# PE in program order while attention runs beside the first expert layer, and ELU's parts marked urgent there

## Chip, core and metric

The kernel runs on one core of one Trainium2 chip. Its engines are PE (TensorE, the matmuls, with PEld for the loads of the stationary operand), DVE (VectorE), ACT (ScalarE), POOL (GpSimd) and SP (SyncE, which here only issues DMAs). The metric is device time in microseconds of one execution, lower is better.

## What is computed

Three stages follow each other. The first is a linear attention with decay over two batches of 8 heads, 768 positions and head size 64, written for blocks of 64:

```python
for b in range(nb):
    qb, kb, vb = (q[:, :, sl], k[:, :, sl], v[:, :, sl])
    intra = np.einsum('bhic,bhjc->bhij', qb, kb) * Dmask[None]
    intra = np.einsum('bhij,bhjd->bhid', intra, vb)
    inter = np.einsum('bhid,bhde->bhie', qb * lam_pow[None], kv_state)
    out[:, :, sl] = intra + inter
    kv_state = lam_block * kv_state + np.einsum('bhsd,bhse->bhde', kb_dec, vb)
```

Its output, reshaped to 1536 tokens of 512, goes through two dense layers of inner size 2048, the first with ELU and the second with softplus:

```python
h = x @ w_in;  g = np.where(h > 0.0, h, np.exp(np.minimum(h, 0.0)) - 1.0);  x = g @ w_out
h = x @ w_in2; g = np.maximum(h, 0.0) + np.log1p(np.exp(-np.abs(h)));      x = g @ w_out2
```

## The kernel before

Attention works on 12 chunks g of 128 positions (all 8 heads; chunks 0 to 5 are the first batch), and has three kinds of matmul groups on PE, eight or sixteen small matmuls each, that use the 128 x 128 array in three different forms. `s(g)`, line 228, multiplies k with q (64 rows by 128 columns of the array); `t(g)`, line 272, makes the state from k and v (128 rows by 64 columns); `x(g)`, lines 245 and 250, makes the output, first from the state (64 by 64), then from the scores (128 by 64). DVE masks the scores (line 231), adds the state (278), and splits the output into a high and a low part together with ACT (xh on ACT, line 260; xl on DVE, line 261). POOL scales q in place after s(g) (203), ACT scales k and v's partner k for the state (209, head by head).

A dense layer goes over 3 tiles of 512 tokens and 16 pieces of the inner size, 48 steps n. `m1(n)`, lines 343 to 345, is 12 matmuls of 512 columns that need the split token tile and weight chunk n's high and low part; ELU follows (`pointwise1` on ACT, `pointwise2` on DVE line 378, ACT line 383 and POOL line 384); `m2(n)`, line 408, is 12 more matmuls, issued two steps later. These use the whole array. Steps 0 to 3 work on token tile 0 (chunks 0 to 3), steps 4 to 7 on tile 1 (chunks 4 to 7) with the same weight chunks 0 to 3.

A weight chunk arrives as float64 words and is converted by two operations on ACT and six on DVE (lines 98 to 120; the last is line 120, which writes the low part). Eight chunks are converted while attention runs; weight chunks 4 to 7 are used only later. In the traces' names wh_215 belongs to chunk 0, wh_271 to 1, wh_343 to 2, wh_413 to 3, and wl_482 to 4.

A scheduler orders the instructions of an engine, except inside `manual_schedule`, where the engines that are named keep the order in which the code is written. The first part (setup, 13 attention slots, then steps 0 to 7) keeps only SP in the order of the code; from step 8 on PE, ACT, POOL and SP keep it. `high_priority(k)` makes the scheduler prefer what stands under it. A step's code is: a slot t, m1(n), its ELU, a slot s, m2(n-2), a slot x. SP's queue is in the order of the code in both kernels: the load of weight chunk k+2 waits until line 120 of chunk k has run, and the loads of later q, k and v stand behind it.

Of the kernel before, what the change touches and what calls it, by code (L numbers as in the profile page):

```python
# [1 line left out]

# [1 line left out]

# [32 lines left out]
def body(ctx, tc, lamc, ident, attqk, attkv, w1, w2, out):  # L37
# [41 lines left out]
    def w_ops(count, start):  # L79

        while count:
            if not flight:
                if not start or wnext[1] == len(wqueue):
                    return
                flight.append(split_w(wqueue[wnext[1]]))
                wnext[1] += 1
            if next(flight[0], True):
                flight.pop()
            count -= 1
# [44 lines left out]
    def setup():  # L134
        A.preload_act_table_set("natural_log_exp_and_others")
        V.memset(zero, 0.0)

        ps = ps_h.tile([P, TT], F32, tag="h", name="warm")
        for i in range(9):
            T.matmul(ps[:, :P], zero, zero, start=True, stop=True)  # L140
        nc.sync.dma_start(out=lam_t, in_=lamc)
        nc.sync.dma_start(out=id_t, in_=ident)
        att_load(0)
        att_load_kv(0)
        load_w()
        att_load(1)
        att_load_kv(1)
        for g in (2, 3):
            att_load(g)
            att_load_kv(g)  # L150
        load_w()

    def decays():
        for h in range(H):
            V.tensor_tensor_scan(
                out=dmask[:, h % 2, h // 2, :], data0=lam_t[:, h:h + 1].to_broadcast([P, P]), data1=id_t,
                initial=0.0, op0=ALU.mult, op1=ALU.add,
            )
        for e in range(2):
            V.tensor_copy(kdecay[:, e::2], dmask[:, e, :, P - 1])  # L160
        for p in range(NPAIR):
            V.tensor_tensor_scan(
                out=qpow[:, p, :], data0=lam_t[:, H + p:H + p + 1].to_broadcast([P, P]), data1=zero,
                initial=1.0, op0=ALU.mult, op1=ALU.add,
            )
# [39 lines left out]
    def att_prep_k(g):  # L205
        if g < NCHUNK and g % CPB < CPB - 1:
            for h in range(H):
                k = at[g][2][:, D * h:D * h + D]
                A.activation(out=k, in_=k, func=AF.Copy, scale=kdecay[:, h:h + 1])
# [82 lines left out]
    def flush():  # L292
        while deferred:
            deferred.pop(0)()

    def att_slot(ahead=None):

        with tc.high_priority(ahead):
            att_part()
# [32 lines left out]
    def m1(n):  # L332
        u, c = order[n]
        layer, t, begin, _ = units[u]
        fc = layer * NF + c
        if c == begin:
            xcur[u % 2] = (xh[t], xl[t])
        h, l = xcur[u % 2]
        pool, tag = (ps_a, "a") if late and n % 2 else (ps_h, "h")
        ps = pool.tile([P, TT], F32, tag=tag, name="hps")  # L340
        for k in range(KD):
            o = slice(P * k, P * k + P)
            T.matmul(ps, wh[fc, 0][:, o], h[:, k, :], start=(k == 0), stop=False)  # L343
            T.matmul(ps, wh[fc, 0][:, o], l[:, k, :], start=False, stop=False)  # L344
            T.matmul(ps, wl[fc, 0][:, o], h[:, k, :], start=False, stop=(k == KD - 1))  # L345
        return ps


    mid = {}

    def pointwise1(n, ps):
        if units[order[n][0]][0] == 0:
            v = tp.tile([P, TT], F32, tag="v", name="v")
            A.activation(out=v, in_=ps, func=AF.Relu, scale=-1.0)  # L354
            A.activation(out=v, in_=v, func=AF.Exp, scale=-1.0)  # L355
            mid[n] = ps, v, None
        else:

            lp = late["tp"]
            e = lp.tile([P, TT], F32, tag="e", name="e")  # L360
            l = lp.tile([P, TT], F32, tag="l", name="l")
            u = lp.tile([P, TT], F32, tag="u", name="u")
            A.activation(out=e, in_=ps, func=AF.Abs)  # L363
            A.activation(out=e, in_=e, func=AF.Exp, scale=-1.0)
            A.activation(out=u, in_=e, func=AF.Copy, bias=1.0)
            A.activation(out=l, in_=u, func=AF.Ln)  # L366
            mid[n] = ps, l, (u, e)

    def pointwise1b(n):
        if n in mid and mid[n][2]:  # L370
            u, e = mid[n][2]
            V.scalar_tensor_tensor(out=u, in0=u, scalar=-1.0, in1=e, op0=ALU.add, op1=ALU.subtract)  # L372

    def pointwise2(n):
        ps, v, u = mid.pop(n)
        if u is None:

            V.scalar_tensor_tensor(out=v, in0=v, scalar=-1.0, in1=ps, op0=ALU.add, op1=ALU.max)  # L378
        else:
            V.tensor_tensor(out=v, in0=v, in1=u[0], op=ALU.subtract)  # L380
            V.scalar_tensor_tensor(out=v, in0=ps, scalar=0.0, in1=v, op0=ALU.max, op1=ALU.add)
        g = gp.tile([P, 2, TT], F32R, tag="g", name="g")
        A.activation(out=g[:, 0], in_=v, func=AF.Copy)  # L383
        G.tensor_tensor(out=g[:, 1], in0=v, in1=g[:, 0].bitcast(F32), op=ALU.subtract)  # L384
        gt[n] = g

    split = []
    ahead = []

    def split_x():  # L390
        if split:
            t, y, m = split.pop(0)
            A.activation(out=xh[t][:, m, :], in_=y, func=AF.Copy)
            G.tensor_tensor(out=xl[t][:, m, :], in0=y, in1=xh[t][:, m, :].bitcast(F32), op=ALU.subtract)
# [49 lines left out]
    def close_attention():  # L444
        actx.close()
        late["acc"] = ctx.enter_context(tc.tile_pool(name="late", bufs=1, reuse_waits="tile"))
        late["tp"] = ctx.enter_context(tc.tile_pool(name="ltp", bufs=2, reuse_waits="tile"))

    def w_start(n):

        j = n - 13
        return wnext[1] < 8 or j >= 0 and j % 2 == 0 and j % 24 < 16

    def step(n):
        last = len(order) - 1
        pieces = 4 if n < 4 else 2
        att_slot(100)
        if n <= last:
            pointwise1(n, ahead.pop() if ahead else m1(n))
        if n == last - 1:  # L460
            ahead.append(m1(last))
        if n - 1 in mid:
            pointwise2(n - 1)
        if n <= last:
            pointwise1b(n)
        split_x()
        w_ops(pieces, wnext[1] < 8)
        att_slot(100)
        if n >= LAG:
            m2(n - LAG)  # L470
        att_slot(100)
        flush()
        if not slots and not late:
            close_attention()
        w_ops(pieces, w_start(n))

    ET = mybir.EngineType


    with tc.manual_schedule(engines={ET.SP}):  # L480
        setup()
        decays()
        att_prep_k(0)
        while len(slots) > 3 * (NCHUNK - TT // P) - 1:
            if not spare:
                spare.extend([f"y{m}" for m in range(KD)])
            att_slot()
            w_ops(2, True)
        spare.clear()
        for n in range(8):  # L490
            step(n)
    with tc.manual_schedule(engines={ET.PE, ET.Activation, ET.Pool, ET.SP}):
        for n in range(8, len(order) + LAG):
            step(n)
# [47 lines left out]
```

## Time and profile before

| | us |
|---|---|
| median of 3 runs | 636.27 (635.71 to 636.72) |
| the profiled execution, own time | 634.41 |
| its span, first to last instruction | 632.6 |
| PE busy | 610.4 |
| DVE busy | 408.5 |
| ACT busy | 341.1 |
| POOL busy | 173.6 |

The own time is 1.8 us above the span, and 1.9 us below the median of the runs. Busy PE is no measure of PE at its peak: a matmul counts as busy while the engine changes the form of the array or runs at half its clock.

### The profile page before, as it was taken

To read this page: it belongs to the slowest core of one execution; us is meant where nothing else is said; L and a number is where in the kernel's file an instruction comes from. 1 tells how busy PE (TensorE), PEld (TensorE's weight loads), DVE (VectorE), ACT (ScalarE), POOL (GpSimd) and SP (SyncE) were. 2 spreads that over 40 slices of the span, in tenths; PEclk is the share of its full clock that TensorE was granted. 3 is DMA by queue.
4 is the path that set the end of the run, shared out by engine and by line. 5 is a ranking of instruction groups with operands and counts; after the bars stand their busy time and mean duration, and the time that the engine had idled before them with its cause. 6 is when DMAs were issued, how large, how long until landed. Compare 5 with 4: busy or idle time off the path is not lost.

```text
span 632.6 us, 7785 instructions
## 1 busy us (share of the span) xinstructions
PE 610.4 (96%) x3026; PEld 495.7 (78%) x3026; DVE 408.5 (65%) x469; ACT 341.1 (54%) x577; POOL 173.6 (27%) x130
## 2 busy tenths in 40 slices
PE   7979879999999999999999998999999999999997
PEld 6666667788888888888888886888878888888885
DVE  6387992311275867221787899556999996555654
ACT  4435462334356554333556677466787775655553
POOL 1222221212223222224335235322223232222222
PEclk9669966999999999999999999999999999999999
DMA  8505465100013231100113213000231300100101
GB/s 318 218 20 223 192 265 184 51 0 1 0 68 117 84 132 68 66 1 1 67 68 129 75 62 111 23 1 1 71 129 67 132 2 1 67 1 1 67 0 67
DMA packets 10117, 49.86 MB, mean 79 GB/s; under 512 B 1248, under 2 KB 1376, under 8 KB 5984
## 3 DMA queue, kind: packets, MB, share of 16 engines
q1 hardware_dynamic: 10080, 49.36, 21.0%
q8 instruction: 24, 0.39, 0.3%
q14 instruction: 13, 0.11, 0.0%
HBM read 46.21 MB, written 3.15 MB: 78 GB/s over the span
## 4 chain that ended last, share of the span: by engine, by line
PE 82%; issue 6%; DVE 5%; ACT 2%; POOL 2%; DMA 1%; SPq 0%; POOLq 0%; DVEq 0%; ACTq 0%
PE y L408 37%; PE hps L345 13%; PE hps L343 13%; PE hps L344 13%; PE sps L228 3%; PE xps L245 2%; PE xps L250 1%; PE stps L272 1%; POOL g L384 1%; DMA qk<-attqk 1%; DVE t L109 1%; POOL qk L203 1%; DVE wl L120 1%; DVE u L372 1%; DVE raw L99 1%
## 5 line engine op out<-in xcount | busy, mean ns | idle before, releaser
L343 PE MATMUL hps<-xh,wh 128*128 128x512 f32 x384 | 151.6, 395 | 1.2 <-ACT xh L260 1.2
L344 PE MATMUL hps<-xl,wh 128*128 128x512 f32 x384 | 150.9, 393 | 0.0
L345 PE MATMUL hps<-xh,wl 128*128 128x512 f32 x384 | 150.8, 393 | 0.0
L408 PE MATMUL y<-wh,g 128*128 128x512 f32 x384 | 120.6, 392 | 3.2 <-POOL g L384 2.8
L408 PE MATMUL y<-g,wh 128*128 128x512 f32 x384 | 119.2, 390 | 3.3 <-POOL g L384 1.9
L384 POOL TENSOR_TENSOR g<-v,g 128x512 fp32r<-128x512 f32 x48 | 65.9, 1374 | 201.4 <-ACT g L383 201.4
L384 POOL TENSOR_TENSOR g<-l,g 128x512 fp32r<-128x512 f32 x48 | 68.6, 1428 | 185.2 <-ACT g L383 163.8
L354 ACT ACTIVATE v<-hps 128x512 f32<-128x512 f32 x48 | 28.7, 599 | 120.2 <-PE hps L345 120.1
L378 DVE SCALAR_TENSOR_TENSOR v<-v,hps 128x512 f32<-128x512 f32 x48 | 32.9, 684 | 91.5 <-ACT v L355 89.3
L408 PEld LDWEIGHTS y<-wh,g 128*128 128x128 f32 x384 | 72.1, 188 | 21.5 <-POOL g L384 6.3
L408 PEld LDWEIGHTS y<-g,wh 128*128 128x128 f32 x384 | 72.0, 188 | 19.6 <-POOL g L384 2.8
L343 PEld LDWEIGHTS hps<-xh,wh 128*128 128x128 f32 x384 | 72.8, 190 | 17.4 <-ACT xh L260 1.8
L344 PEld LDWEIGHTS hps<-xl,wh 128*128 128x128 f32 x384 | 72.6, 189 | 15.6 <-issue 0.2
L345 PEld LDWEIGHTS hps<-xh,wl 128*128 128x128 f32 x384 | 72.6, 189 | 15.4 <-issue 0.3
L372 DVE SCALAR_TENSOR_TENSOR u<-u,e 128x512 f32<-128x512 f32 x48 | 44.0, 917 | 56.1 <-ACT l L366 56.1
L408 PE MATMUL y<-wl,g 128*128 128x512 f32 x192 | 74.8, 389 | 0.0
L408 PE MATMUL y<-g,wl 128*128 128x512 f32 x192 | 74.7, 389 | 0.0
L363 ACT ACTIVATE e<-hps 128x512 f32<-128x512 f32 x48 | 28.7, 598 | 69.6 <-PE hps L345 69.6
L380 DVE TENSOR_TENSOR l<-l,u 128x512 f32<-128x512 f32 x48 | 61.7, 1286 | 3.7
L120 DVE SCALAR_TENSOR_TENSOR wl<-raw,r 128x1024 fp32r<-128x1024 uint32 x32 | 46.7, 1459 | 0.8
L119 ACT ACTIVATE wh<-t 128x1024 fp32r<-128x1024 f32 x32 | 33.8, 1056 | 20.0 <-DVE t L109 19.7
L408 PEld LDWEIGHTS y<-g,wl 128*128 128x128 f32 x192 | 36.1, 188 | 7.4
(58 smaller groups left out, 740.6 us busy)
## 6 DMA issues: line engine op xcount, KB each, us to landing
raw<-w SPq DMA_DIRECT2D x32, 1024.0 KB, 4.8
qk<-attqk SPq DMA_DIRECT2D x11, 512.0 KB, 5.7
kv<-attkv SPq DMA_DIRECT2D x10, 512.0 KB, 6.1
out<-yacc SPq DMA_DIRECT2D x8, 256.0 KB, 2.0
early<-attkv SPq DMA_DIRECT2D x2, 512.0 KB, 11.5
out<-o SPq DMA_DIRECT2D x4, 256.0 KB, 2.4
early<-attqk SPq DMA_DIRECT2D x1, 512.0 KB, 11.6
id_t<-ident SPq DMA_DIRECT2D x1, 64.0 KB, 2.0
```

What stands on the lines that cost most here:

```text
L119: A.activation(out=hi, in_=t, func=AF.Copy)
L120: V.scalar_tensor_tensor(out=lo, in0=high, scalar=2.0 ** -43, in1=r, op0=ALU.mult, op1=ALU.mult)
L343: T.matmul(ps, wh[fc, 0][:, o], h[:, k, :], start=(k == 0), stop=False)
L344: T.matmul(ps, wh[fc, 0][:, o], l[:, k, :], start=False, stop=False)
L345: T.matmul(ps, wl[fc, 0][:, o], h[:, k, :], start=False, stop=(k == KD - 1))
L354: A.activation(out=v, in_=ps, func=AF.Relu, scale=-1.0)
L363: A.activation(out=e, in_=ps, func=AF.Abs)
L372: V.scalar_tensor_tensor(out=u, in0=u, scalar=-1.0, in1=e, op0=ALU.add, op1=ALU.subtract)
L378: V.scalar_tensor_tensor(out=v, in0=v, scalar=-1.0, in1=ps, op0=ALU.add, op1=ALU.max)
L380: V.tensor_tensor(out=v, in0=v, in1=u[0], op=ALU.subtract)
L384: G.tensor_tensor(out=g[:, 1], in0=v, in1=g[:, 0].bitcast(F32), op=ALU.subtract)
L408: T.matmul(yps[m], a, b, start=(c == begin and i == 0), stop=(c == end - 1 and i == 2))
```

## The change

PE joins SP in the order of the code for the first part, up to step 7. Of a step's ELU the three parts are put under `high_priority(200)` in these steps, and the call of m1 is moved out of that block.

```diff
--- before.py
+++ after.py
@@ -1,4 +1,4 @@
-from contextlib import ExitStack
+from contextlib import ExitStack, nullcontext
 
 import numpy as np
 
@@ -455,14 +455,16 @@
         last = len(order) - 1
         pieces = 4 if n < 4 else 2
         att_slot(100)
-        if n <= last:
-            pointwise1(n, ahead.pop() if ahead else m1(n))
+        ps = None if n > last else ahead.pop() if ahead else m1(n)
         if n == last - 1:
             ahead.append(m1(last))
-        if n - 1 in mid:
-            pointwise2(n - 1)
-        if n <= last:
-            pointwise1b(n)
+        with tc.high_priority(200) if n < 8 else nullcontext():
+            if n <= last:
+                pointwise1(n, ps)
+            if n - 1 in mid:
+                pointwise2(n - 1)
+            if n <= last:
+                pointwise1b(n)
         split_x()
         w_ops(pieces, wnext[1] < 8)
         att_slot(100)
@@ -477,7 +479,8 @@
     ET = mybir.EngineType
 
 
-    with tc.manual_schedule(engines={ET.SP}):
+
+    with tc.manual_schedule(engines={ET.SP, ET.PE}):
         setup()
         decays()
         att_prep_k(0)
```

PE, in the attention slots ahead of step 0. The names: stps is t(g), sps_256 and sps_257 are s(2), xps is x(1), early is data of chunk 2. Before, the scheduler mixes the groups:

```order
L245 MATMUL xps<-qk,state 64x128
L228 MATMUL sps_256<-qk 128x128
L272 MATMUL stps<-kv 64x64
L245 MATMUL xps<-qk,state 64x128
L228 MATMUL sps_257<-qk 128x128
L228 MATMUL sps_256<-qk 128x128
L245 MATMUL xps<-qk,state 64x128
L272 MATMUL stps<-kv 64x64
L228 MATMUL sps_257<-qk 128x128
L245 MATMUL xps<-qk,state 64x128
L272 MATMUL stps<-kv 64x64
L272 MATMUL stps<-early 64x64
```

With the change each group stands whole:

```order
L272 MATMUL stps<-kv 64x64 x8
L228 MATMUL sps_256<-qk 128x128
L228 MATMUL sps_257<-qk 128x128
L228 MATMUL sps_256<-qk 128x128
L228 MATMUL sps_257<-qk 128x128
L228 MATMUL sps_256<-qk 128x128
L228 MATMUL sps_257<-qk 128x128
L228 MATMUL sps_256<-qk 128x128
L228 MATMUL sps_257<-qk 128x128
L245 MATMUL xps<-qk,state 64x128 x8
L250 MATMUL xps<-sc,kv 64x128 x8
L272 MATMUL stps<-early 64x64 x8
```

The three kinds are no longer mixed. Counted over the whole part, the form of the array changes 95 times before and 48 times after, up to the last attention matmul.

PE, at step 2. Before, t(6) (stps) comes after m1(2), m1(3) and m2(0) to m2(3) (wh_413 is weight chunk 3), mixed with s(7):

```order
L408 MATMUL y_675<-g,wh_413 128x512 x2
L408 MATMUL y_675<-g,wl_414 128x512
L272 MATMUL stps<-kv 64x64
L228 MATMUL sps_658<-qk 128x128
L272 MATMUL stps<-kv 64x64
L228 MATMUL sps_658<-qk 128x128
L272 MATMUL stps<-kv 64x64
L228 MATMUL sps_658<-qk 128x128
L272 MATMUL stps<-kv 64x64
L228 MATMUL sps_658<-qk 128x128
L272 MATMUL stps<-kv 64x64 x4
L228 MATMUL sps_659<-qk 128x128 x4
```

With the change x(5) and t(6) come first, then m1(2) (wh_343 is weight chunk 2):

```order
L245 MATMUL xps<-qk,state 64x128 x8
L250 MATMUL xps<-sc,kv 64x128 x8
L272 MATMUL stps<-kv 64x64 x8
L343 MATMUL hps<-xh_199,wh_343 128x512
L344 MATMUL hps<-xl_200,wh_343 128x512
L345 MATMUL hps<-xh_199,wl_344 128x512
L343 MATMUL hps<-xh_199,wh_343 128x512
L344 MATMUL hps<-xl_200,wh_343 128x512
L345 MATMUL hps<-xh_199,wl_344 128x512
```

So m1(2), m1(3) and m2(0) to m2(3), which stood ahead of t(6), now stand behind it, one group in each place of the step.

DVE, between the last operations of weight chunks 3 and 4 (wl_414 and wl_482). sps_564 and sps_565 are s(6), xl_519 the low part of tile 1:

```order
L120 SCALAR_TENSOR_TENSOR wl_414<-raw,r 128x1024
L261 TENSOR_TENSOR xl_519<-xps,xh_518 128x4x128
L231 TENSOR_TENSOR sc<-sps_564,dmask 128x512
L99 TENSOR_SCALAR raw<-raw 128x1024
L106 TENSOR_SCALAR t<-r 128x1024
L101 SCALAR_TENSOR_TENSOR raw<-raw 128x1024
L231 TENSOR_TENSOR sc<-sps_565,dmask 128x512
L109 SCALAR_TENSOR_TENSOR t<-r,t 128x1024
L261 TENSOR_TENSOR xl_519<-xps,xh_518 128x4x128
L112 TENSOR_SCALAR r<-t 128x1024
L99 TENSOR_SCALAR raw<-raw 128x1024
L120 SCALAR_TENSOR_TENSOR wl_482<-raw,r 128x1024
```

and with the change:

```order
L120 SCALAR_TENSOR_TENSOR wl_414<-raw,r 128x1024
L99 TENSOR_SCALAR raw<-raw 128x1024
L106 TENSOR_SCALAR t<-r 128x1024
L101 SCALAR_TENSOR_TENSOR raw<-raw 128x1024
L109 SCALAR_TENSOR_TENSOR t<-r,t 128x1024
L261 TENSOR_TENSOR xl_519<-xps,xh_518 128x4x128
L112 TENSOR_SCALAR r<-t 128x1024
L120 SCALAR_TENSOR_TENSOR wl_482<-raw,r 128x1024
L378 SCALAR_TENSOR_TENSOR v<-v,hps 128x512
L231 TENSOR_TENSOR sc<-sps_564,dmask 128x512
L231 TENSOR_TENSOR sc<-sps_565,dmask 128x512
```

The masking of s(6), one xl and the ELU part of step 1 now stand behind chunk 4's last operation. From step 8 on every engine's order is as before.

## Rows read from the trace of the kernel before

**Rows 1.** The page's head, and the first line of its part 4, the chain of work that ended last (shares of the span by engine).

```profile
span 632.6 us, 7785 instructions
...
PE 82%; issue 6%; DVE 5%; ACT 2%; POOL 2%; DMA 1%; SPq 0%; POOLq 0%; DVEq 0%; ACTq 0%
```

**Rows 2.** Stretches cut where the granted clock changes. Columns: the stretch in us, its length, then busy us of PE, PEld, DVE, ACT and POOL with the count of instructions, then PEclk (1.00 is 2.4 GHz, 0.50 is 1.2 GHz), the DMA share and GB/s.

```profile
0.00:13.65 13.65, 10.21 (x86) 9.05 (x86) 8.74 (x22) 5.75 (x15) 1.59 (x6) 1.00 0.80 302
13.65:27.25 13.60, 12.65 (x74) 8.74 (x74) 6.24 (x9) 5.34 (x19) 3.30 (x3) 0.50 0.79 320
27.25:37.55 10.30, 7.79 (x102) 6.15 (x98) 7.80 (x10) 5.00 (x15) 5.07 (x4) 1.00 0.01 2
37.55:47.75 10.20, 8.94 (x45) 6.79 (x46) 7.69 (x11) 2.52 (x3) 0.00 (x0) 0.50 0.14 42
47.75:85.30 37.55, 33.56 (x215) 25.01 (x213) 32.94 (x39) 22.08 (x36) 8.16 (x6) 1.00 0.60 227
85.30:105.80 20.50, 17.33 (x118) 13.92 (x117) 12.17 (x16) 7.00 (x22) 6.34 (x6) 0.50 0.56 205
105.80:125.60 19.80, 19.80 (x204) 14.88 (x203) 6.29 (x10) 6.75 (x19) 4.40 (x4) 1.00 0.23 80
```

**Rows 3.** PE's instructions in order of time in the first 45 us. Columns here and in the other views in order of time: start in us, us, engine, line, operation, out<-in, rows*columns of the array in use, shape, count of passes (a matmul on float32 shows as two), and in brackets the idle time before and what ended it.

```profile
11.63 1.16 PE L228 MATMUL sps<-qk 64*128 64x128 f32 x16 [1.81 <-DMA qk<-attqk]
...
15.12 1.11 PE L245 MATMUL xps<-qk,state 64*64 64x128 f32 x6 [0.95 <-POOL qk L203]
...
20.47 0.69 PE L245 MATMUL xps<-qk,state 64*64 64x128 f32 x2
21.09 0.80 PE L228 MATMUL sps<-qk 64*128 64x128 f32 x4
...
40.61 1.97 PE L250 MATMUL xps<-sc,early 128*64 128x128 f32 x16
```

**Rows 4.** ACT in order of time: the scaling of k of chunk 1, head by head.

```profile
12.81 2.02 ACT L209 ACTIVATE kv<-kv,kdecay 128x64 f32<-128x64 f32 x8 [1.34 <-DMA kv<-attkv]
```

**Rows 5.** PE in order of time from 55 to 97 us: groups of one form at 2.4 GHz (the first five) and at 1.2 GHz (the last two).

```profile
56.34 0.50 PE L343 MATMUL hps<-xh,wh 128*128 128x512 f32 x1
...
57.24 1.09 PE L245 MATMUL xps<-qk,state 64*64 64x128 f32 x16
58.26 1.09 PE L250 MATMUL xps<-sc,kv 128*64 128x128 f32 x16
59.28 0.50 PE L343 MATMUL hps<-xh,wh 128*128 128x512 f32 x1
...
83.50 0.45 PE L272 MATMUL stps<-kv 128*64 128x64 f32 x8
...
91.54 2.41 PE L228 MATMUL sps<-qk 64*128 64x128 f32 x16 [0.99 <-DVE xl L261]
94.72 1.94 PE L245 MATMUL xps<-qk,state 64*64 64x128 f32 x14 [0.78 <-DVE sc L231]
```

**Rows 6.** DVE's groups by line from 0 to 130 us. Columns: busy us and mean ns of one, then idle us before them and what ended it.

```profile
L231 DVE TENSOR_TENSOR sc<-sps,dmask 128x512 f32<-128x512 f32 x24 | 15.9, 684 | 10.5 <-PE sps L228 10.4
L120 DVE SCALAR_TENSOR_TENSOR wl<-raw,r 128x1024 fp32r<-128x1024 uint32 x8 | 11.2, 1397 | 0.2
L109 DVE SCALAR_TENSOR_TENSOR t<-r,t 128x1024 uint32<-128x1024 uint32 x8 | 10.8, 1352 | 0.0
L101 DVE SCALAR_TENSOR_TENSOR raw<-raw 128x1024 uint32<-128x1024 uint32 x8 | 9.7, 1214 | 0.0
L261 DVE TENSOR_TENSOR xl<-xps,xh 128x512 fp32r<-128x512 f32 x12 | 8.2, 686 | 8.5 <-ACT xh L260 8.5
L99 DVE TENSOR_SCALAR raw<-raw 128x1024 uint32<-128x1024 uint32 x8 | 7.7, 958 | 0.8 <-ACT r L98 0.8
L112 DVE TENSOR_SCALAR r<-t 128x1024 uint32<-128x1024 uint32 x8 | 6.0, 746 | 0.1
L106 DVE TENSOR_SCALAR t<-r 128x1024 uint32<-128x1024 uint32 x8 | 5.9, 736 | 0.0
L378 DVE SCALAR_TENSOR_TENSOR v<-v,hps 128x512 f32<-128x512 f32 x6 | 4.1, 678 | 4.4 <-ACT v L355 4.4
L278 DVE TENSOR_TENSOR state<-stps,faded 128x256 f32<-128x256 f32 x8 | 3.4, 422 | 19.1 <-PE stps L272 14.5 <-PE xps L245 2.4 <-PE xps L250 2.2
```

**Rows 7.** DVE in order of time: the xl of chunk 3, the first ELU part on DVE, and the last operations (L120) of weight chunks 4 and 7.

```profile
43.26 0.69 DVE L261 TENSOR_TENSOR xl<-xps,xh 128x512 fp32r<-128x512 f32 x1 [0.84 <-ACT xh L260]
...
49.94 0.69 DVE L378 SCALAR_TENSOR_TENSOR v<-v,hps 128x512 f32<-128x512 f32 x1 [1.85 <-ACT v L355]
...
69.62 1.21 DVE L120 SCALAR_TENSOR_TENSOR wl<-raw,r 128x1024 fp32r<-128x1024 uint32 x1
...
92.45 1.52 DVE L120 SCALAR_TENSOR_TENSOR wl<-raw,r 128x1024 fp32r<-128x1024 uint32 x1
```

**Rows 8.** The DMA queue of SP in order of time: the loads of weight chunks 2 and 3, merged; the time is that until the second was issued.

```profile
18.27 27.17 SPq L75 DMA_DIRECT2D raw<-w  x2
```

**Rows 9.** The DMA issues of the first 130 us, the line of the loads of q and k: count, KB each, median us to landing.

```profile
qk<-attqk SPq DMA_DIRECT2D x11, 512.0 KB, 5.7
```

**Rows 10.** The chain of work from 130 to 150 us: one group of twelve matmuls with 512 columns.

```profile
136.28 2.72 PE y L408 x12
```

**Rows 11.** PE in order of time: the first matmul behind the sixth second-matmul group, m2(5).

```profile
138.84 0.39 PE L343 MATMUL hps<-xh,wh 128*128 128x512 f32 x1
```

## The prediction

> **What bounds the kernel now.** I read the page's head and its chain first: the end hangs on PE for 82% of the span [rows 1]. From 125 us on PE has no idle time worth naming and the change moves nothing behind step 7, so the whole question is when PE has done the work of steps 0 to 7. A mark for that is the first matmul behind m2(5), where m1(0) to m1(7), m2(0) to m2(5) and all attention matmuls are done: 138.84 us [rows 11]. How many us this mark moves, that many the end moves.
>
> Next the windows, cut where the granted clock changes [rows 2]. Before 126 us there are three kinds of stretch. From 13.65 to 47.75 us PE walks through the attention slots, two of its three stretches at 1.2 GHz. From 47.75 to 85.30 us the clock is 2.4 GHz, and DVE is busy 32.94 of 37.55 us, nearly as much as PE's 33.56; PE waits for DVE's conversion of weights and DVE waits for little. From 85.30 to 105.80 us PE is at 1.2 GHz again, with little else than attention left to do while DVE has only 12.17 us of work; the matmuls of the dense layer that could have stood between have been used up.
>
> The mixing of forms is seen in PE's order of time [rows 3]: two matmuls of x(1) at 20.47, then four of s at 21.09. The two took 0.62 us from start to start; sixteen passes of line 250 in one form, also at 1.2 GHz, took 1.97 (40.61 to 42.58, where x(3) ends), 0.25 for the same two. So a change of form costs some 0.4 us at 1.2 GHz. At 2.4 GHz three matmuls of m1 between two groups of another form took 0.90 us (56.34 to 57.24), against 12 in 2.72 without a change [rows 5, 10], 0.23 each: 0.22 a change.
>
> The Trainium skill, "TensorEngine Tiling (Array Packing)", the notes on what a change of tiling mode does, says that such a change drains TensorE; the trace agrees with the 0.22. Forty-seven changes fewer by that price alone would give 10.3 us, 626.0 us; nothing below is built on this, since many of these changes stand where PE waits anyway.
>
> **Part 1: the attention slots, to the end of x(3).** Nothing moves up to t(1), which ACT paces head by head: k of chunk 1 is scaled from 12.81 to 14.83 [rows 4], so t(1) ends near 15.0, and the clock has just gone to 1.2 GHz. Prices of whole groups at 1.2 GHz: s 2.41; x 2.2 (fourteen passes of line 245 took 1.94) + 1.97, together 4.2; at 2.4 GHz: s 1.16, x 1.02 + 1.02 = 2.04, t 0.45 + 0.22 for the form, 0.7 [rows 3, 5]. No row shows t in one piece at 1.2 GHz: between 0.7 and twice that, I take 1.0. With them: s(2) 15.0 to 17.4, x(1) to 21.6, t(2) to 22.6. Here I choose: PE, no more broken up, gets 2.4 GHz back at about this point, because it works without a pause from 15 us on, while before it had changed form every one to four matmuls. Then s(3) 1.16, x(2) 2.04, t(3) 0.7, s(4) 1.16, x(3) 2.04, 7.1 us, and one wait for POOL's scaling of q, as the 0.95 ahead of x(1) [rows 3]: **x(3) ends at 30.6** instead of 42.58. Bounds: 28.6 with the clock back behind s(2) and no wait; 32 if it is back only at 27.25 as before; 36.8 if all of it runs at 1.2 GHz (22.6 + 2.41 + 4.2 + 1.0 + 2.41 + 4.2).
>
> **Part 2: DVE, which sets the pace up to x(6).** Two halves of xl (0.69 each) bring it to 31.9. By the order of the instructions, DVE then has, up to line 120 of chunk 4, one of line 278, four of 112, three of 99, four of 120, three each of 101, 106 and 109, one of 378, two of 231 and one of 261. By the means of [rows 6] that is 24.5 us. (Before, from 43.95 to 70.83 [rows 7], it was 26.9 with more masks and ELU in between.) Chunk 4 is converted at 56.4. Then stands the operation that the change brought ahead: `pointwise2(1)`, line 378, now ahead of the masks of s(6). An ELU part waits for ACT; before, the first of them waited 1.85 [rows 7]. I take one such wait, with none and two, 0 and 3.7, as bounds. Behind it, up to the second mask of s(7): two of 378, four of 231, three each of 99 and 106, two each of 101, 109, 112 and 120, one 261 and one state operation (0.42), 19.7 us. So the mask that x(6) needs is done at 56.4 + 1.85 + 19.7 = **77.9**, and chunk 7 converted 5.8 us later, 83.7 instead of 93.97.
>
> What is covered by this. SP's queue is in order: chunk 3's load goes at the end of line 120 of chunk 1 (before at 45.44, [rows 8]; now near 35.3 by the same counting), and q and k of chunk 5 behind it land 5.7 us after their issue [rows 9], 41.5. PE, out of m1(0) by 34.5, waits some 7 us there. s(5) is then done at 42.7; its masks stand on DVE behind line 112 of chunk 3, which by the same counting ends at 46.5, so 3.8 us of cover hide this wait. The loads of chunk 6 stand behind line 120 of chunk 4 in the same way, ACT's scaling of it behind the cast of chunk 5: 11.2 us after 56.4 it can be used, then m1(2), s(7) and m2(0), so x(6) could start 18.2 after chunk 4 (20.8 if that runs at 1.2 GHz), against DVE's 21.55. This cover is thin, 0.7 to 3.3 us; if it fails, x(6) is late by as much as is missing.
>
> **Part 3: PE from x(6) to the mark.** The second half of x(6) is 1.02. Steps 3 to 6 are t 0.7, m1 2.72 + 0.22, s 1.16, m2 2.94, x 2.04 = 9.78 each; step 7, to the mark, m1(7), x(11) and m2(5), 7.92. Together 1.02 + 39.1 + 7.9 = 48.1 us. Within a step the mask of s lies behind m2 and ELU behind a step, so I add only 0.7 for the xl of x(7), which m1(4), the first of tile 1, needs. The mark: 77.9 + 48.1 + 0.7 = **126.7**, 12.1 us earlier than 138.84.
>
> The profiled execution takes 634.41 (span 632.6 and 1.8 around it), so 622.3; it lies 1.86 below the median of the runs, so the median becomes **624.2**.
>
> With all bounds low (x(3) at 28.6, no ELU wait, a tenth less on DVE's 44.2 and no stall at m1(4)) the mark is near 118, the median 615; with all high (36.8, 3.7 and 2 us of missing cover) near 137, 634.
>
> **Rivals.**
> (a) *The slots stay at 1.2 GHz.* x(3) ends at 36.8 and all behind it is 6.2 later: gain 5.9, 630.4 us. For it: the clock fell at 13.65 after PE had been busy for most of the time before (10.21 of 13.65), and stayed down with PE busy 12.65 of 13.60, so a busy PE alone did not keep it [rows 2]. Against: from 27.25 it was back even with the forms mixed.
> (b) *Steps 2 to 7 run at 1.2 GHz* (slower than before). The prologue ends earlier, PE then waits 7 us for q and k of chunk 5 and several times a few us for DVE in steps 1 and 2; before, it had matmuls of m1 and m2 to put there. The stretch from 85.30 to 105.80 shows what such a PE gets: 17.33 busy of 20.50, and half the clock. There twelve matmuls cost twice 2.72; the 48 us of part 3 would become up to 96, for a gain that turns into a loss as soon as some 12 us of its full-clock work runs at half. Median 624.2 + 24 = 648 if half of it does. Against: from 47.75 to 85.30 PE was idle 4 of 37.55 us with m1, m2, s and x in turn, and kept 2.4 GHz [rows 2]; in part 3 it has hardly a pause. The Trainium skill, "TensorE: Matmul & The Clock Gate", section "Why this matters for your kernels", warns of idle gaps between bursts of matmuls; the trace agrees so far as that the idle share before the fall at 85.30 and in it was higher than in part 3's sum.
> (c) *Nothing is gained at the mark.* DVE's masks, now behind the ELU parts, or the thin cover of chunk 6 give back 12 us; that takes four waits of three us, where the rows show 1.85 as the largest for line 378. 636 us.
> (d) *More than forecast*: below 617, if the clock is full from 20 us on and ELU never waits; the sum with all lows is 615.
>
> **How the numbers follow.** The forecast, 618 to 629, gets 0.60; (a) 0.18; (b) 0.09; (c) 0.05; (d) 0.08. The likeliest, 624.2, is the predicted time. For 8 in 10 the range takes the forecast, (a) and the upper part of (d): 617 to 632. What a measurement of this kernel can tell from no change is about 0.2%, 1.3 us. Faster is the sum of the forecast, (a), (d) and a little of (c), 0.87; same 0.04; slower, (b) and a remnant of (c), 0.09.
>
> **What the profile after would show.** Right: groups of eight or sixteen in PE's rows up to 30 us; x(3) ending between 29 and 32 and the clock back before 27; line 120 of chunk 4 near 56 and of chunk 7 near 84; PE's largest wait, some 7 us, between 34 and 42 for a DMA of q and k; x(6) near 78 and the mark near 127, 2.4 GHz between; from the mark to the end as many us as before. Wrong would make it: the clock at 1.2 GHz from 13.65 on to 35 (a); a second stretch of 1.2 GHz behind 50 us (b), first to be looked for between 56 and 78, where PE waits for DVE; a wait of DVE of over 3 us at line 378 or at a mask (c); t(6) ending after DVE's mask of s(7) (the cover).

## The result, and the profile after

The changed kernel takes **620.73 us** (median of 3 runs, 620.02 to 621.14) against 636.27: a ratio of 0.9755 with a 95% interval of 0.9733 to 0.9777, so 15.5 us faster. The profiled execution is the one of 620.73 us; its span is 618.9 against 632.6 [rows 1]. The prediction said 624.2 within 617 to 632, so the direction and the order of size held and the gain was 3.5 us larger than the forecast.

The page's head, the busy line of the engines, the clock in 40 slices, and the first line of the chain of work, of the changed kernel:

```profile
span 618.9 us, 7786 instructions
...
PE 586.3 (95%) x3026; PEld 480.0 (78%) x3026; DVE 408.2 (66%) x469; ACT 340.6 (55%) x577; POOL 171.6 (28%) x130
...
PEclk9967899999999999999999999999999999999999
...
PE 80%; DVE 9%; issue 4%; ACT 3%; DMA 2%; POOL 2%; SPq 0%; DVEq 0%; ACTq 0%; POOLq 0%
```

In the chain DVE's share has risen from 5 to 9% and PE's fallen from 82 to 80 [rows 1]: what is left ahead of the mark hangs more on DVE. DVE has as much work as before (408.2 against 408.5 us busy) and PE 24 us less busy time (586.3 against 610.4), for the same matmuls: a busy PE holds its half clock and its changes of form, as the table of before says of that figure.

Stretches of the changed kernel, cut by what PE does, with the columns of [rows 2]:

```profile
14.40:37.00 22.60, 16.41 (x206) 13.40 (x204) 20.70 (x29) 12.39 (x33) 6.85 (x6) 0.92 0.49 187
37.00:52.50 15.50, 6.26 (x49) 5.34 (x50) 14.87 (x16) 5.57 (x7) 3.32 (x2) 0.56 0.64 238
...
59.20:69.30 10.10, 7.20 (x51) 5.78 (x48) 10.06 (x12) 4.47 (x11) 1.06 (x1) 0.67 0.45 178
...
77.00:90.00 13.00, 12.29 (x116) 9.60 (x113) 8.64 (x11) 6.95 (x20) 4.53 (x5) 1.00 0.59 189
90.00:125.00 35.00, 35.00 (x302) 27.70 (x301) 9.77 (x16) 14.61 (x35) 8.34 (x7) 1.00 0.17 59
```

Against [rows 2]: the attention slots, up to 37 us here, run at a mean granted clock of 0.92, and the poor stretch at 1.2 GHz from 85.30 to 105.80 us is gone; from 77 us on the clock is full. But half-clock stretches did not vanish: 37 to 52.5 and 59.2 to 69.3 us show 0.56 and 0.67. In both DVE is busy nearly without a pause (14.87 of 15.50, 10.06 of 10.10).

PE in order of time, the rows that answer to the prediction's steps (columns as in [rows 3]):

```profile
14.40 1.16 PE L228 MATMUL sps<-qk 64*128 64x128 f32 x16
16.31 1.09 PE L245 MATMUL xps<-qk,state 64*64 64x128 f32 x16 [0.74 <-DVE sc L231]
17.33 1.09 PE L250 MATMUL xps<-sc,kv 128*64 128x128 f32 x16
...
27.35 1.09 PE L250 MATMUL xps<-sc,early 128*64 128x128 f32 x16
...
31.83 0.66 PE L344 MATMUL hps<-xl,wh 128*128 128x512 f32 x1 [2.19 <-DVE xl L261]
...
40.63 2.08 PE L228 MATMUL sps<-qk 64*128 64x128 f32 x16 [4.42 <-DMA qk<-attqk]
48.31 1.97 PE L245 MATMUL xps<-qk,state 64*64 64x128 f32 x16 [5.61 <-DVE sc L231]
...
58.85 1.57 PE L245 MATMUL xps<-qk,state 64*64 64x128 f32 x16 [2.47 <-DVE sc L231]
...
65.23 2.15 PE L272 MATMUL stps<-kv 128*64 128x64 f32 x16 [2.90 <-ACT kv L209]
...
76.34 1.09 PE L250 MATMUL xps<-sc,kv 128*64 128x128 f32 x16 [0.89 <-DVE sc L231]
...
88.41 0.51 PE L343 MATMUL hps<-xh,wh 128*128 128x512 f32 x1 [0.23 <-ACT xh L260]
89.40 0.50 PE L344 MATMUL hps<-xl,wh 128*128 128x512 f32 x1 [0.48 <-DVE xl L261]
...
125.06 0.39 PE L343 MATMUL hps<-xh,wh 128*128 128x512 f32 x1
```

x(1) now stands in two whole groups (16.31, 17.33). x(3) ends at 28.44 (27.35 + 1.09). m1(0) waits 2.19 us for DVE's xl, s(5) 4.42 for the load of q and k, x(4) 5.61 for DVE's masks, x(5) 2.47 for them again, and t(6) 2.90 for ACT's scaling of k (65.23). x(6), which has matmuls of line 250 alone because chunk 6 begins the second batch, starts at 76.34 behind a wait of 0.89 for DVE's mask of s(7). The first matmul behind m2(5), the mark, comes at **125.06** instead of 138.84 [rows 11], 13.78 earlier. From there to the end of the span it is 493.8 us in both kernels (632.6 − 138.84 and 618.9 − 125.06): all that the two profiled executions differ by lies ahead of the mark. Their spans differ by 13.7 us; the rest of the 15.5 is the distance of the profiled execution of before to its median.

DVE of the changed kernel in order of time, and behind it two of POOL's operations:

```profile
31.09 0.68 DVE L261 TENSOR_TENSOR xl<-xps,xh 128x512 fp32r<-128x512 f32 x1
...
43.42 2.29 DVE L101 SCALAR_TENSOR_TENSOR raw<-raw 128x1024 uint32<-128x1024 uint32 x1
...
54.60 1.22 DVE L120 SCALAR_TENSOR_TENSOR wl<-raw,r 128x1024 fp32r<-128x1024 uint32 x1
57.42 0.69 DVE L378 SCALAR_TENSOR_TENSOR v<-v,hps 128x512 f32<-128x512 f32 x1 [1.59 <-ACT v L355]
...
61.33 1.21 DVE L101 SCALAR_TENSOR_TENSOR raw<-raw 128x1024 uint32<-128x1024 uint32 x1
...
75.61 1.28 DVE L231 TENSOR_TENSOR sc<-sps,dmask 128x512 f32<-128x512 f32 x2
76.81 1.98 DVE L101 SCALAR_TENSOR_TENSOR raw<-raw 128x1024 uint32<-128x1024 uint32 x1
...
81.54 1.23 DVE L120 SCALAR_TENSOR_TENSOR wl<-raw,r 128x1024 fp32r<-128x1024 uint32 x1
```

```profile
42.82 1.80 POOL L203 TENSOR_TENSOR qk<-qk,qpow 128x512 f32<-128x512 f32 x1 [2.34 <-PE sps L228]
...
76.42 1.28 POOL L384 TENSOR_TENSOR g<-v,g 128x512 fp32r<-128x512 f32 x1 [2.49 <-ACT g L383]
```

The xl of x(3) starts at 31.09, 2.65 us behind x(3)'s end: DVE was still on chunk 1. Chunk 4's last operation ends at 55.82, line 378 behind it waits 1.59 us for ACT, the two masks of s(7) end at 76.89 and chunk 7's last operation at 82.77, against 93.97 before [rows 7].

### The profile page after: what moved, and what is told of

It is laid out like the page before. It is cut to its first block, busy times and chain, and to the rows that moved or that the text cites. A ratio compares the mean times of both kernels' runs of the same rounds, so it can differ in the third digit from the quotient of the medians.

```text
span 618.9 us, 7786 instructions
## 1 busy us (share of the span) xinstructions
PE 586.3 (95%) x3026; PEld 480.0 (78%) x3026; DVE 408.2 (66%) x469; ACT 340.6 (55%) x577; POOL 171.6 (28%) x130
## 4 chain that ended last, share of the span: by engine, by line
PE 80%; DVE 9%; issue 4%; ACT 3%; DMA 2%; POOL 2%; SPq 0%; DVEq 0%; ACTq 0%; POOLq 0%
PE y L408 37%; PE hps L344 13%; PE hps L343 13%; PE hps L345 13%; PE xps L250 1%; PE xps L245 1%; DVE t L109 1%; DVE raw L101 1%; DMA qk<-attqk 1%; DVE raw L99 1%; DVE t L106 1%; PE sps L228 1%; DVE u L372 1%; POOL g L384 1%; DMA raw<-w 1%
## 5 line engine op out<-in xcount | busy, mean ns | idle before, releaser
L120 DVE SCALAR_TENSOR_TENSOR wl<-raw,r 128x1024 fp32r<-128x1024 uint32 x32 | 46.1, 1439 | 0.7
L119 ACT ACTIVATE wh<-t 128x1024 fp32r<-128x1024 f32 x32 | 33.8, 1057 | 22.7 <-DVE t L109 22.3
```

The costliest lines, as they stand in the source:

```text
L119: A.activation(out=hi, in_=t, func=AF.Copy)
L120: V.scalar_tensor_tensor(out=lo, in0=high, scalar=2.0 ** -43, in1=r, op0=ALU.mult, op1=ALU.mult)
```

## The experiments

Three theories were told apart. **D**: with whole groups the attention slots end some 12 us earlier, DVE's conversion, which sets the pace up to x(6), starts that much earlier, and PE's order in the steps keeps dense matmuls for the time behind. **F**: the gain is the sum of the 47 changes of form that are saved. **G**: the slots don't matter; what counts is only that dense matmuls are kept for the stretch behind 80 us. Ratios are to the kernel before, timed again beside each experiment; its medians there were 634.2 to 634.6 us, against 636.27 beside the changed kernel, whose ratio is 0.9755. From the mark to the end every profiled execution here takes 493.7 to 494.1 us, so they can also be compared at the mark. There the experiments look better against the changed kernel than by their ratios, by 0.4 to 3.5 us (except the second and third, whose profiled executions lie 3 to 4 us above their medians), so a difference of some 2 us between an experiment and the changed kernel is not settled by either.

### One half of the change at a time

The ELU's mark undone:

```diff
-        with tc.high_priority(200) if n < 8 else nullcontext():
+        with nullcontext():
```

> PE in the order of the code as in the changed kernel, ELU's parts not marked urgent: the second part of the change undone. PE's order is that of the changed kernel to the row (48 changes of form); DVE and ACT have a few ELU parts later. All three theories (D: the attention slots end 12 us earlier and DVE's conversion chain with them; F: 47 changes of form fewer; G: the dense matmuls are kept for the stretch behind 80 us) put the gain into PE's order: 619 to 623 us. If ELU's marking carries part of the gain, 624 or more.

Measured: 619.65 us, 0.9770 (0.9750 to 0.9789). The interval overlaps that of the changed kernel; marking ELU's parts urgent carries nothing that can be seen.

PE's order undone, the ELU's mark kept:

```diff
-    with tc.manual_schedule(engines={ET.SP, ET.PE}):
+    with tc.manual_schedule(engines={ET.SP}):
         setup()
```

> ELU's parts marked urgent, PE left to the scheduler: the first part of the change undone. 96 changes of form, attention slots mixed as before. D, F and G: 635 to 638 us, no difference from before beyond 0.3%. If the urgent ELU were what lets the dense matmuls follow, 630 or less.

Measured: 634.68 us, 1.0021 (0.9996 to 1.0047). The gain is PE's order alone.

### The order in the slots alone, in the steps alone

```diff
         spare.clear()
+    with tc.manual_schedule(engines={ET.SP}):
         for n in range(8):
             step(n)
```

> PE in the order of the code only in the 13 attention slots ahead of step 0; in steps 0 to 7 the scheduler orders it again (94 changes of form, 24 of them ahead of the first dense matmul). D: x(3) ends near 29, DVE's chain runs as in the changed kernel, chunk 7 is converted near 83, and the mark follows some 45 us later as before: 622 to 626 us. F: as many changes of form as before, so 634 to 637. G: the scheduler puts the dense matmuls early again and a stretch with attention alone comes back: 630 or more.

Measured: 626.15 us, 0.9868 (0.9843 to 0.9894): 8.4 us, more than half of the gain, with 94 changes of form against 95 before. F falls; D's 622 to 626 is met but for 0.15 us. Of this experiment, the stretch of half clock (columns as in [rows 2]), PE in order of time inside it, and DVE's last operation of chunk 7:

```profile
68.00:102.00 34.00, 31.22 (x180) 24.55 (x182) 17.70 (x23) 10.18 (x29) 5.67 (x6) 0.50 0.47 181
```

```profile
89.55 0.69 PE L272 MATMUL stps<-kv 128*64 128x64 f32 x6
90.17 0.79 PE L228 MATMUL sps<-qk 64*128 64x128 f32 x2
```

```profile
84.62 1.71 DVE L120 SCALAR_TENSOR_TENSOR wl<-raw,r 128x1024 fp32r<-128x1024 uint32 x1
```

DVE's chain is early as D says (chunk 7 done at 86.33, the changed kernel 82.77). x(6) starts at 75.50, no later than in the changed kernel. But PE has used its dense matmuls up, and from 68 to 102 us it runs at 1.2 GHz with t and s mixed (89.55, 90.17), so that the mark comes at 134.50. G is right in that part, though not in this size: the profiled execution is the longest of the four (630.02 us, mean granted clock 0.970). The two shortest, 624.71 and 625.01 us, have 0.984, no less than the changed kernel's 0.981, and are still 4 us longer than it. What those 4 us are, the changes of form in the steps or the order itself, was not taken apart.

The other way round, the slots scheduled and the steps in the order of the code:

```diff
-    with tc.manual_schedule(engines={ET.SP, ET.PE}):
+    with tc.manual_schedule(engines={ET.SP}):
         setup()
 ...
         spare.clear()
+    with tc.manual_schedule(engines={ET.SP, ET.PE}):
         for n in range(8):
             step(n)
```

> PE in the order of the code only in steps 0 to 7; the 13 attention slots stay mixed (64 changes of form, 30 of them ahead of the first dense matmul). D: x(3) ends near 42 as before, DVE's chain is as late as before, chunk 7 is converted at 92 to 95, and the mark comes 42 us later: 631 to 636 us. F: 31 changes of form fewer, two thirds of the gain: 624 to 628. G: the dense matmuls stand behind the chain as in the changed kernel: 622 to 627.

Measured: 631.20 us, 0.9954 (0.9941 to 0.9967), a gain of 2.9 us. G said 622 to 627 and F 624 to 628, both fall; D's range holds. DVE in order of time, the xl of chunk 3 and chunk 7's last operation:

```profile
42.75 0.69 DVE L261 TENSOR_TENSOR xl<-xps,xh 128x512 fp32r<-128x512 f32 x1 [0.39 <-ACT xh L260]
...
90.92 1.23 DVE L120 SCALAR_TENSOR_TENSOR wl<-raw,r 128x1024 fp32r<-128x1024 uint32 x1
```

The xl of chunk 3 comes at 42.75, as late as before (43.26, [rows 7]), and chunk 7's last operation at 90.92. So of 15.5 us the slots alone give 8.4, the steps alone 2.9, and 4.2 come only with both (3.3, with some 2 us of uncertainty, if the first experiment, timed beside these two, stands for the whole). An early DVE chain is worth more where PE has dense matmuls left for the time behind it.

### Less work for DVE ahead of x(6)

If DVE sets when x(6) starts, taking work from it there must move the mark with no change in PE's order.

```diff
-        pieces = 4 if n < 4 else 2
+        pieces = 0 if n < 4 else 4 if n < 8 else 2
```

In the code of steps 0 to 3 no conversion is issued now, in steps 4 to 7 four operations at each of two places (not two, as the expectation says). The scheduler, which orders DVE, still puts chunks 4 and 5 early (line 120 at 59.19 and 66.94); line 120 of chunks 6 and 7 runs at 97.31 and 111.08 instead of 70.59 and 81.54.

> The changed kernel with one number changed: in steps 0 to 3 no operation of the conversion of weights is issued, and from step 4 two at a time, so that chunks 6 and 7 are converted between 85 and 115 us, where DVE was mostly idle. D (DVE's conversion sets when x(6) can start): about 8.5 us of DVE's work leave the stretch before the second mask of s(7); x(6) comes 5 to 8 us earlier, the mark as much: 613 to 616 us. If loads and ACT's scaling of k of chunk 6 are next in line right behind DVE, 618 to 620. F (changes of form): 48 as in the changed kernel, no difference, 620 to 621.

Measured: 614.94 us, 0.9699 (0.9675 to 0.9723), about 3.5 us below the changed kernel's ratio and faster than both kernels; in the predicted 613 to 616. DVE in order of time (the masks of s(7)), the stretch from 90 us on (columns as in [rows 2]), and PE in order of time (x(6) and the mark):

```profile
68.08 0.68 DVE L231 TENSOR_TENSOR sc<-sps,dmask 128x512 f32<-128x512 f32 x1
...
69.44 0.68 DVE L231 TENSOR_TENSOR sc<-sps,dmask 128x512 f32<-128x512 f32 x1
```

```profile
90.00:120.00 30.00, 29.33 (x264) 23.36 (x265) 20.06 (x27) 15.69 (x30) 9.01 (x6) 1.00 0.44 159
```

```profile
70.54 1.09 PE L250 MATMUL xps<-sc,kv 128*64 128x128 f32 x16
...
120.11 0.39 PE L343 MATMUL hps<-xh,wh 128*128 128x512 f32 x1
```

The masks of s(7) end at 70.12 instead of 76.89, x(6) starts at 70.54 instead of 76.34, the mark is at 120.11 instead of 125.06. x(6) no longer waits for DVE: PE comes to it straight from m2. In 90 to 120 us DVE now works 20.06 us, and PE's way from x(6) to the mark is 49.6 us against 48.7, so this costs 0.9 us at most. The edit does not only take work from DVE: the loads of k and v of chunk 6 are no longer behind a weight chunk that waits for chunk 4 (issued at 53.19 instead of 56.75), and t(6) starts at 60.77 instead of 65.23. The same without the ELU's mark:

```diff
-        pieces = 4 if n < 4 else 2
+        pieces = 0 if n < 4 else 4 if n < 8 else 2
-        with tc.high_priority(200) if n < 8 else nullcontext():
+        with nullcontext():
```

> As the one before, and in addition ELU's parts are not marked urgent. D: the marking puts line 378 and its wait for ACT ahead of masks, so without it the masks come 0 to 2 us earlier: 612 to 615 us, 0 to 2 us below the one before. If the marking matters for PE's wait in m2, it is 1 us slower than the one before.

Measured: 615.65 us, 0.9696 (0.9669 to 0.9723), no difference from the one before; a gain of 0 to 2 us from leaving ELU's parts unmarked was not seen.

### What a change of form costs, by place

```diff
+        if g < 4 and not first:
+            todo = [(f, *h) for h in heads for f in (from_state, from_scores)]
+        for f, p, e in todo:
+            f(p, e)
```

Here `from_state` and `from_scores` are the matmuls of the two loops of `att_x`, and `todo` otherwise holds first all of one and then all of the other.

> The changed kernel with the two kinds of matmul in x(1), x(2) and x(3), in the slots ahead of step 0, written head by head (state, scores, state, scores) instead of eight and eight: 42 changes of form more, the order of the groups untouched. A change costs 0.23 us at 2.4 GHz by the rows of the third experiment (two passes of line 245 and two of 250 in turn, 0.36 from start to start, against 0.13 in a group). F: 42 x 0.23 = 9.7 us, 630 us. D: x(1) to x(3) end up to 9.7 us later in sum, of which DVE had 2.8 us of other work at the end of x(3) and 1 to 2 us of idle time between: 624 to 628 us; more if the clock goes to half.

Measured: 626.05 us, 0.9872 (0.9848 to 0.9896), 7.4 us above the changed kernel's ratio, in D's 624 to 628 and below F's 630. A stretch of the slots (columns as in [rows 2]) and PE in order of time (lines 244 and 249 are the two kinds of x here, 349 to 351 m1):

```profile
14.40:28.00 13.60, 12.77 (x105) 7.58 (x101) 9.67 (x14) 6.39 (x19) 4.10 (x4) 1.00 0.70 278
```

```profile
16.46 0.43 PE L244 MATMUL xps<-qk,state 64*64 64x128 f32 x2
16.82 0.43 PE L249 MATMUL xps<-sc,kv 128*64 128x128 f32 x2
...
36.19 0.27 PE L249 MATMUL xps<-sc,early 128*64 128x128 f32 x1
...
37.88 0.50 PE L350 MATMUL hps<-xl,wh 128*128 128x512 f32 x1 [0.23 <-DVE xl L267]
```

Two passes take 0.36 us from start to start. In the third experiment, from which the expectation took that figure, two of line 245 stood between passes of line 272, not 250 (26.55 to 26.91). x(3) ends 8.0 us later (36.19 + 0.27 against 28.44), m1(0) goes on 6.1 us later (37.88 against 31.83), and the mark comes 5.2 us later (130.24). The granted clock stays at 1.00 although the form changes every two passes.

The same with `g > 6` in the place of `g < 4`:

> The same mixing in x(7) to x(11) alone, where PE has no idle time: 70 changes of form more. Each at 0.23 us lies on the path by both theories: 16.3 us, 637 us. If less than 633, a change is cheaper than the rows of mixed groups say, or part of it lies beside the load of the stationary operand.

Measured: 638.83 us, 1.0075 (1.0047 to 1.0102); this loses all of the gain and more. PE in order of time, of x(7) and at the mark:

```profile
84.23 0.43 PE L244 MATMUL xps<-qk,state 64*64 64x128 f32 x2
84.59 0.43 PE L249 MATMUL xps<-sc,kv 128*64 128x128 f32 x2
...
142.32 0.39 PE L349 MATMUL hps<-xh,wh 128*128 128x512 f32 x1
```

The mark comes 17.3 us later (142.32), 0.25 a change, near the 0.23 of the rows; by the ratios it is 20 us, 0.29 a change. A change of form costs its full price where PE has no idle time. In the slots, of the ten us that 42 changes make, two or three were hidden by the ratios and about half by the mark.

### The waits of step 0 and the clock there

Loads of chunk 5 ahead of weight chunk 3 in SP's queue:

```diff
-            w_ops(2, True)
+            w_ops(1 if len(slots) == 30 else 2, True)
```

> The changed kernel with one operation of conversion less in one slot, so that in SP's queue the loads of q, k and v of chunk 5 stand ahead of the load of weight chunk 3 instead of behind it. PE's wait of 4.4 us ahead of s(5) should go. D: that wait is hidden, since the masks of s(5) stand on DVE behind chunk 3's line 112 and PE then waits 5.6 us for them anyway: 619 to 621 us, within 2 us of the changed kernel. If the wait for q and k is on the path, the mark comes 4 us earlier: 616 to 617. Weight chunk 3 itself arrives later, which can cost DVE a wait: then 621 to 624.

Measured: 617.93 us, 0.9755 (0.9729 to 0.9781), the changed kernel's ratio. PE in order of time:

```profile
36.09 1.16 PE L228 MATMUL sps<-qk 64*128 64x128 f32 x16
...
61.25 2.15 PE L272 MATMUL stps<-kv 128*64 128x64 f32 x16 [10.71 <-ACT kv L209]
...
71.54 1.09 PE L250 MATMUL xps<-sc,kv 128*64 128x128 f32 x16
...
121.95 0.39 PE L343 MATMUL hps<-xh,wh 128*128 128x512 f32 x1
```

s(5) starts at 36.09 without a wait, 4.5 us earlier than in the changed kernel, and PE waits 10.71 us ahead of t(6) instead. By the ratio nothing is gained, as D said. The trace does not bear that out: x(6) starts at 71.54 without a wait and the mark comes 3.1 us earlier than in the changed kernel. The scheduler also gave DVE another order here (the masks of s(5) at 38.09, ahead of the end of chunk 2), so this is no clean test of the wait alone, and whether it was fully hidden stays open.

Matmuls of zeros in PE's waits, 36 each:

```diff
+    def keep(count):
+        ps = ps_h.tile([P, TT], F32, tag="h", name="keep")
+        for i in range(count):
+            T.matmul(ps[:, :P], zero, zero, start=True, stop=True)
 ...
+        if n == 0:
+            keep(36)
```

(once behind m1 and once behind the slot of s.)

> The changed kernel with matmuls of zeros, which no result uses, in PE's two waits of step 0: 36 behind m1(0) and 36 behind s(5), some 4 us each. The clock, which fell to 1.2 GHz there (40 to 52 us), should stay at 2.4, and s(5), x(4) and the start of m1(1) run at full speed. D: x(4) is 2 us shorter and m1(1) ends 2 us earlier, so that line 378 of step 1 no longer waits 1.59 us for ACT; the mark 1 to 2 us earlier: 618.5 to 620. If the clock in DVE's stretch is what sets the time: 615 to 617. If the zeros get in the way of s(5): 621 to 623.

Measured: 618.56 us, 0.9744 (0.9719 to 0.9769). The same on top of the fifth experiment:

> The fifth experiment (chunks 6 and 7 converted later) together with the matmuls of zeros. There PE waits 4.5 us ahead of s(5) and 5.5 ahead of x(4) and runs at 1.2 GHz from 41 to 53 us. D: 1 to 3 us less than the fifth experiment, 612 to 614; if the clock there is fully hidden, 614.5 to 615.5.

Measured: 617.84 us, 0.9735 (0.9714 to 0.9756): 2.3 us worse than the fifth experiment, where I had expected 1 to 3 better. PE in order of time in the tenth experiment:

```profile
35.85 8.20 PE L393 MATMUL keep<-zero 128*128 128x128 f32 x72
...
45.07 8.30 PE L393 MATMUL keep<-zero 128*128 128x128 f32 x72
53.30 1.09 PE L245 MATMUL xps<-qk,state 64*64 64x128 f32 x16
```

Thirty-six took 8.2 us, twice what I had reckoned; the second batch held x(4) back to 53.30, 5 us later than in the changed kernel. The tenth experiment nevertheless lost nothing. The five us may have been given back by the full clock, or by DVE, which went on with the conversion meanwhile (line 120 of chunk 5 at 60.67 instead of 65.41); the runs do not tell which. The intervals of the eleventh and the fifth just overlap, and why the eleventh came out longer was not followed further. Eighteen each, otherwise as the eleventh:

```diff
-            keep(36)
+            keep(18)
```

> The experiment before with 18 matmuls of zeros instead of 36 at each of the two places. Thirty-six took 8.2 us, twice what I had reckoned, and held s(5) and x(4) up by 3 and 5 us; eighteen should take 4.1 and fit into the waits of 4.5 and 5.5 us. D with the clock partly on the path: s(5) and x(4) at 2.4 GHz and on time, 612 to 614 us, 1 to 3 below the fifth experiment. If the half clock there is hidden behind DVE: 614.5 to 616, as the fifth experiment.

Measured: 613.24 us, 0.9671 (0.9637 to 0.9706). PE in order of time:

```profile
35.66 4.18 PE L393 MATMUL keep<-zero 128*128 128x128 f32 x36
...
48.63 1.09 PE L245 MATMUL xps<-qk,state 64*64 64x128 f32 x16
```

x(4) runs at full clock and starts at 48.63. The point lies 1.8 us below the fifth experiment's, as D with the clock partly on the path said, but the intervals overlap: whether the zeros gain anything beside the later conversion stays open. It is the lowest ratio of all, and like the fifth experiment below both kernels.

## Why the prediction was right, and where it was off

**Where the gain lies.** Right: it lies ahead of the mark, and from the mark on nothing changed (493.8 us in both).

**Part 1, the slots.** Forecast: x(3) ends at 30.6 (28.6 to 32 if the clock returns). It ended at 28.44. The low bound was added up wrongly: with the clock back behind s(2) and no wait, the prediction's own prices give 17.4 + 2.04 + 0.7 + 7.1 = 27.2. The step that was mis-sized is "s(2) 15.0 to 17.4, x(1) to 21.6" at half clock; they took 14.40 to 18.42, at 2.4 GHz. Of these 3.2 us a wait of 2.06 for POOL ahead of x(2) (22.70), where the sum had 0.95, took back 1.1.

That the clock would be up was a choice, and its reason, that PE is "no more broken up", is not borne out: the seventh experiment changes the form every two passes in the same slots and kept 1.00, with PE busy 12.77 of 13.60 us, while before it was 0.50 at 12.65 of 13.60 [rows 2]. Why it fell before stays open, and that the choice came out was in part luck.

The 2.2 us gained on the forecast were worth 0.1 at DVE, which ended xl at 31.77 (forecast 31.9), because it had chunk 1 to finish first. (The "two halves" of xl are one operation, 31.09, behind 0.60 us of ACT's xh.) I had let x(3) release DVE; from there on it was DVE's own work that bound. The seventh experiment says so from the other side: 8.0 us later at x(3) is 6.1 at m1(0). So does the tenth: in its slots x(2) ran at 1.2 GHz and x(3) ended at 30.85, and yet its mark, 123.99, is not later.

**Part 2, DVE's chain.** Right within about a us at each place: chunk 4 at 55.82 (56.4), the wait of line 378 there 1.59 (1.85), masks of s(7) 76.89 (77.9), chunk 7 at 82.77 (83.7). Up to chunk 4 two errors cancel in part: line 378 of step 0 waited 1.35 us as well (37.53), which the sum did not have, and the operations took 22.7 us in place of 24.5.

The cover of s(5) held: s(5) was done at 42.71, and DVE took its masks at 47.48, behind line 112 of chunk 3, without a wait. PE's wait ahead of it was 4.42 and not 7, since m1(0) ran partly at 1.2 GHz and ended at 36.2, and q and k landed 0.9 us earlier than reckoned. PE's largest wait was not this one but the 5.61 for those masks. The cover of chunk 6 held by 0.89 us, which is all that x(6) waited for DVE; the prediction had 0.7 to 3.3. The sign it named for this cover, t(6) ending behind DVE's mask of s(7), could not come, as s(7) stands behind t(6) on PE.

PE's own way to x(6) hung on the conversion too: t(6) waited for ACT, which scaled k of chunk 6 at 64.84, behind its casts for chunks 6 and 5 (62.87 and 63.90), and the one for chunk 5 could not start before DVE's line 109 had ended (63.68). That the conversion sets x(6) is shown by the fifth experiment, which moved both ways at once; how much lies on the masks and how much on this second way is not told apart.

**Part 3, PE from x(6) to the mark.** Forecast 48.1 + 0.7; measured from 76.34 to 125.06, 48.7 us, m1(4)'s two waits of 0.23 and 0.48 in it (88.41 and 89.40).

**The sum.** The mark was forecast at 126.7 and came at 125.06, 1.6 us of the 3.5 by which the gain was too small: about 1 from the masks and 0.5 from x(6), which started ahead of the second mask's end. The other 1.9 is what I carried over from before, the distance of its profiled execution to its median (634.41 against 636.27); the profiled execution after is the median itself. Beside the experiments the kernel before had medians of 634.2 to 634.6, near that execution; with these the gain is 13.5 to 13.9 us. Executions of one kernel scatter by 2 us or more here (609.04 to 616.75 for the twelfth experiment), so a term of that size from one execution says little.

**The rivals.** (a), slots at 1.2 GHz: no, 0.92 of full clock up to 37 us. (b), half clock in steps 2 to 7: half clock did come at 59 to 69 us, in one of the places where I said it had to be looked for, so the sign of (b) appeared and its price did not: there PE waited for DVE and ACT in any case, and in the 48 us behind x(6) the clock was full. The Trainium skill ("TensorE: Matmul & The Clock Gate", section "Why this matters for your kernels") warns of idle gaps between bursts of matmuls; the trace agrees so far as PE was busy only 7.20 of 10.10 us in that stretch. (c): from 28 us to x(6) DVE had no wait over 1.59 us. The "2.4 GHz between" x(6) and the mark was right. The 0.56 from 37 to 52.5 us stood nowhere in the prediction, and no price of it can be shown (the last three experiments).

**The 0.22 a change.** The price was right (0.25 in the eighth experiment), and so was it not to multiply it by 47: the third experiment has 94 changes, as many as before, and more than half of the gain. The Trainium skill, "TensorEngine Tiling (Array Packing)", section "Key Properties", states that a change of tiling mode drains TensorE; the eighth experiment's 0.25 agrees. Summed over all changes the price gave 626.0, which the third and fourth experiments show to be the wrong account.

## To carry to other kernels

Before an order of matmuls is judged by what it costs on PE, ask which engine the stretch waits for: grouping by form in the slots paid here because it let DVE start 12 us earlier. That alone gave more than half of the gain, and the rest came with an order that kept dense matmuls for the time behind. Where another engine's chain binds a stretch, look for the work on it that nobody needs soon: moving two chunks of conversion back gave another 3.5 us with one number. A change of form is worth some 0.25 us at full clock where PE has no idle time, and less in front of a wait.

## What the runs showed of the hardware

DVE's operations on SBUF lengthen when they begin while POOL runs one: line 101 took 2.29 us at 43.42, beside POOL's scaling from 42.82 to 44.62, and 1.98 at 76.81 beside POOL from 76.42 to 77.70, against 1.21 elsewhere (61.33). Both end 1.09 us behind POOL's end, as if they had begun only then. All ten such meetings between 19 and 82 us in this trace show the same, 1.08 to 1.09 us for the long operations and 0.55 to 0.56 for the short ones, while two masks that read PSUM keep their 1.28 us beside POOL (27.56). Five of them lie between the xl of x(3) and the masks of s(7), where DVE sets the pace, and add 4.4 us there (POOL's spans are rough); the sum of part 2 took such lengthened operations in with the means of [rows 6].

Thirty-six passes of zeros, 128 x 128 against 128 columns, took 4.18 us at 2.4 GHz, 0.116 each, where the 64 x 64 passes of x with as many columns took 1.02 for 16 (16.31 to 17.33), 0.064 each.
